# Order of work on VectorE and two value stages in a fused sorting attention and branch mixture, one core

## The chip, the core and the metric

One core of a Trainium2 chip runs the whole kernel. TensorE multiplies matrices into PSUM, VectorE (DVE), ScalarE (ACT) and GpSimd (POOL) do the elementwise work, and SyncE (SP) and GpSimd issue most DMAs. The metric is the device time of one execution in microseconds (us), as the median of several runs.

## The reference

Two parts follow each other. The first is an attention in which blocks of keys and values are first mixed by a matrix that five rounds of row and column normalization make from `sort_net`; the second is a mixture of four two-layer branches over the attention's output.

```python
P = sort_net                                     # 4 batches, 8 heads, 8 x 8
for _ in range(5):
    P = exp(P - max(P)); P = P / rowsum(P); P = P / colsum(P)
k_sorted = einsum('bhij,bhjcd->bhicd', P, k_blocks)
v_sorted = einsum('bhij,bhjcd->bhicd', P, v_blocks)
scores = q_blocks @ k_sorted_blocks.T / sqrt(64) # within each block of 96 tokens
attn = softmax(scores)
x = (attn @ v_sorted_blocks)                     # to (3072 tokens, 512)

p = domain_probs / domain_probs.sum(-1)          # 3072 x 4
out = 0
for e in range(4):
    h = maximum(x @ w1[e], 0)                    # 512 -> 1024
    out += p[:, e:e+1] * (h @ w2[e])             # 1024 -> 512
```

The inputs are q, k, v of shape 4 x 8 x 768 x 64 in fp32; the output is 3072 x 512 in fp32.

## The kernel before, in words

Matmuls run in fp16 and accumulate in fp32. Tokens are handled in twelve chunks of 256: three chunks (`c`) for each of the four batches (`b`). The second layer of a chunk, and for the last chunks the first layer too, is written as seven block products in place of eight (a Strassen-like scheme): sums and differences of blocks are made first (`h_sums`, numbers 1 to 4, on VectorE), the products accumulate in PSUM banks `bankA`, `bankB`, `bankC`, `bankQ`, and VectorE and ScalarE combine them.

The order of all instructions is written out by hand: each engine works through its own instructions in program order, and so does each engine that issues DMAs. The attention of the later batches is cut into stages that are called between pieces of the mixture. The table `PLANS[b]` says after which piece: an entry `(c, n, stage, batch, pair)` runs the stage in chunk `c` at slot `n`. Slots 0 to 5 of chunk (0, 2) follow the six groups of its first layer, slots 6 to 12 the products of its second layer. The stages are:

- `st_v(b, pr)` mixes the values of two heads on TensorE (line 361), ScalarE copies them (L367), and at every second pair six DMAs from SP write them to the tile `vs` (L375), from which `st_a` reads.
- `st_k` mixes keys (L395; ScalarE copies, L404, to `kT`); `st_q` transposes queries by a DMA from SP into `q_ring` (L383); `st_s` makes the scores (L414) and their exponential on ScalarE (L421).
- `st_a` multiplies by the values (L449), and VectorE normalizes (L430, L431). `st_x` transposes the result by a DMA from SP into `xT` (L465), a quarter of `xT` for each pair; the first layer of the next batch reads `xT`.
- `st_n`, `st_lk` and `st_lv` load queries, keys and values by GpSimd.
- `load_p` loads the weights of a chunk, `pb` (L213, SP).

A first layer of a chunk (`chunk_first`) is a row of groups of 16 matmuls (L780), each emptied by VectorE (L786). The attention's tiles in PSUM come from a pool of two buffers, which take turns.

Chunks 0 to 4 are made by `chunk`; the last seven by `last_first` and `last_second`, which use the seven products in the first layer too: the chunk G0 = 5 alone (`lead`), then three pairs. In `last_first` the seven products of a part use the PSUM tiles X, Z (two of each in turn) and Q. `p1` copies Z into X on ScalarE (L1124); `p2` adds a second product into Z, which `finish` empties on VectorE (L1110); `p6`, `p7` and `p4` go on adding into X, with ScalarE copies between (L1131, L1139), and X's last product (`p4`, `a22` by `t4`, the fourth) is emptied by `finish` too. Each turn of the loop makes the first products of part `e` (`now`) and the last ones of part `e - 1` (`prev`).

Of the kernel before, what the change touches and what calls it, by code (L numbers as in the profile page):

```python
# [12 lines left out]
ALU = mybir.AluOpType  # L13
# [4 lines left out]
def kernel(  # L18
# [18 lines left out]
    E = moe_w1.shape[0]  # L37
# [571 lines left out]
    def st_bk(b, qd):  # L609
# [10 lines left out]
            (1, 8, st_s, 1, 1), (1, 8, st_x, 1, 0), (1, 9, st_k, 1, 2), (1, 9, st_q, 1, 3), (1, 9, st_lv, 2, 1),  # L620
            (1, 11, st_a, 1, 1), (1, 12, st_lk, 2, 0),
            (2, 0, st_s, 1, 2), (2, 0, st_x, 1, 1), (2, 0, st_n, 2, 0), (2, 0, st_n, 2, 1), (2, 1, st_k, 1, 3),
            (2, 1, st_n, 2, 2), (2, 1, st_n, 2, 3), (2, 2, st_lk, 2, 1), (2, 3, st_a, 1, 2),
            (2, 4, st_x, 1, 2), (2, 4, st_q, 2, 0), (2, 5, st_s, 1, 3),
            (2, 5, st_q, 2, 1), (2, 6, st_a, 1, 3), (2, 7, st_v, 2, 0), (2, 8, st_x, 1, 3), (2, 8, st_v, 2, 1),
            (2, 9, st_k, 2, 0), (2, 9, st_lv, 3, 0), (2, 9, st_n, 3, 0), (2, 11, st_s, 2, 0), (2, 12, st_q, 2, 2),
        ],
        1: [
# [115 lines left out]
    def h_sums(e, which, own=False, hb=None):  # L744
        h = Hb[:, homes.get(e, e)] if hb is None else hb(e)
        blk = lambda kh, tok: h[:, ds(kh * KH, KH), ds(tok * P, P)]
        sm = [Sb[:, n, e].rearrange("p (f x) -> p f x", f=KH) for n in range(4)]
        tt = nc.vector.tensor_tensor
        if which == 1:
            tt(sm[0], blk(0, 1), blk(1, 1), ALU.add)  # L750
        elif which == 2:
            tt(sm[1], sm[0], blk(0, 0), ALU.subtract)
        elif which == 3:
            tt(blk(0, 1) if own else sm[2], blk(0, 0), blk(0, 1), ALU.subtract)
        else:
            tt(blk(1, 0) if own else sm[3], blk(1, 0), sm[1], ALU.subtract)

    def times(ps, lhs, rhs, es, first=True, done=True, between=None, at=None):

        for e in es:  # L760
            if e == at:
                between()
            for f in range(KH):
                nc.tensor.matmul(  # L764
                    ps, lhs(e, f), Ts[e][rhs][:, f, :],
                    start=(first and e == es[0] and f == 0), stop=(done and e == es[-1] and f == KH - 1),
                    skip_group_check=True,
                )
# [28 lines left out]
    def chunk(b, c, slot, done=()):  # L797

        es = list(range(E)) if b else list(range(1, E))
# [9 lines left out]
        sm = lambda n: (lambda e, f: Sb[:, n, e, ds(f * P, P)])  # L809
# [15 lines left out]
        p1, p5, u2, u3 = [moe.tile([P, DH], F32, name=f"{n}_{b}_{c}", tag=n, bufs=1) for n in ("p1", "p5", "u2", "u3")]  # L825
# [40 lines left out]
        if c:  # L866
            both = ob.rearrange("p (h d) -> p h d", h=2)
            times(bankA, blk(0, 0), "b11", es)
            slot()
            times(bankB, blk(1, 0), "b21", es)  # L870
            slot()
            tt(oa1, bankA, oa1, ALU.add)
            tt(oa1, bankB, oa1, ALU.add)
            h_sums(E - 1, 2)
            times(bankC, blk(1, 1), "n4", es[:1], True, False)
            times(bankQ, sm(0), "t1", es)
            tt(ob2, bankQ, ob2, ALU.add)
            slot()
            for e in es:
                h_sums(e, 3)  # L880
            for e in es:
                h_sums(e, 4)
            times(bankA, sm(1), "t2", es, False)
            tt(oa2, bankA, oa2, ALU.add)
            slot()
            next(sums0)
            times(bankC, blk(1, 1), "n4", es[1:], False)
            tt(ob1, bankC, ob1, ALU.add)
            slot()
            times(bankA, sm(2), "t3", es, False)  # L890
            tt(both, bankA.rearrange("p (o d) -> p o d", o=1).broadcast_to([P, 2, DH]), both, ALU.add)
            slot()
            store(1, ob)
            next(sums0)
            times(bankQ, sm(3), "b22", es, False)
            tt(oa2, bankQ, oa2, ALU.add)
            slot()
            store(0, oa)
            return
# [180 lines left out]
    def seven(g, n):  # L1080

        lead = g == G0
        if lead:
            e, f0, cols = n, 0, P
            pb = pbs[divmod(g, R // 2)]
            home = lambda i, j: Hb[:, e, ds(i * KH, KH), ds(j * P, P)]
            weight = lambda j: pb[:, ds(e, 1), ds(j * P, P)]
            n -= 1
            Q = last["Q"][(0, 0, 1, 3)[e]][:]
        else:  # L1090
            e, f0, cols = n // 2, n % 2 * 2, 2 * P
            home = lambda i, j: (last["H"][e] if j else Hb[:, e])[:, ds(i * KH + f0, 2), :]
            weight = lambda j: pbs[g](j, e)
            Q = last["Q"][n % 4][:]
        m = 512 // cols
        a, t = As[e], Bs[g]
        X, Z = [last[nm][n % len(last[nm])][:] for nm in ("X", "Z")]
        u2, u3, t22, t12 = [last[nm][n % len(last[nm])] for nm in ("u2", "u3", "t22", "t12")]
        tt = nc.vector.tensor_tensor

        def product(dst, lhs, rhs, first=False):
            for f in range(m):
                for k in range(2):
                    nc.tensor.matmul(  # L1104
                        dst[:, ds(f * cols, cols)], a[lhs][:, k, ds((f0 + f) * P, P)], t[rhs][:, k, :],
                        start=(first and f == 0 and k == 0), stop=(f == m - 1 and k == 1), skip_group_check=True,
                    )

        def finish(i, j, src):
            nc.vector.scalar_tensor_tensor(  # L1110
                out=home(i, j), in0=src.rearrange("p (f x) -> p f x", f=m), scalar=0.0,
                op0=ALU.max, in1=weight(j).broadcast_to([P, m, cols]), op1=ALU.mult,
            )

        def finish2(i, j, src):
            nc.scalar.activation(src, src, AF.Relu, bias=0.0, scale=1.0)  # L1116
            nc.gpsimd.tensor_tensor(  # L1117
                home(i, j), src.rearrange("p (f x) -> p f x", f=m),
                weight(j).broadcast_to([P, m, cols]), ALU.mult,
            )  # L1120

        def p1():
            product(Z, "a11", "b11", True)
            nc.scalar.copy(X, Z)  # L1124

        def p5():
            product(Q, "s1", "t1", True)

        def p6():
            product(X, "n2", "n2")  # L1130
            nc.scalar.copy(u2, X)  # L1131

        def p2():
            product(Z, "a12", "b21")
            finish(0, 0, Z)

        def p7():
            product(X, "s3", "t3")
            nc.scalar.copy(u3, X)  # L1139
            tt(t22, Q, u3, ALU.add)  # L1140

        def p4():
            product(X, "a22", "t4")
            finish(1, 0, X)

        def p3():
            product(Q, "s4", "b22")
            tt(t12, Q, u2, ALU.add)  # L1148

        return {  # L1150
            1: p1, 2: p2, 3: p3, 4: p4, 5: p5, 6: p6, 7: p7,
            22: lambda: finish2(1, 1, t22), 12: lambda: finish2(0, 1, t12),
        }

# [5 lines left out]
    def last_first(g, slot=None):  # L1160
        b, c = divmod(g, R // 2)
        lead = int(g == G0)
        if lead:
            chunk_first(b, c, [0], 0, slot)
            last_banks(0)
            last_tmp(g)
            prs = {1: seven(g, 1)}
            prs[1][1]()
            prs[1][5]()
            seven(g, 2)[5]()  # L1170
            prs[1][6]()
            prs[1][2]()
            input_sums(0, 0, True)
            input_sums(0, 1, True)
            last_banks(1)
        else:
            last["e0"][2]()
            prs = {0: last["e0"]}
        N7 = E if lead else 2 * E
        for e in range(1 + lead, N7):  # L1180
            prs[e] = seven(g, e)
        for e in range(1 + lead, N7):
            now, prev = prs[e], prs[e - 1]
            now[1]()
            prev[7]()
            if e > 1 + lead:
                prs[e - 2][12]()
            if not lead or e > 2:
                now[5]()
            now[2]()  # L1190
            now[6]()
            prev[22]()
            prev[4]()
            prev[3]()
        now[7]()
        prev[12]()
        return now

    def last_second(g, now=None, upper=False):

        b, c = divmod(g, R // 2)
        final = g == GN - 1
# [19 lines left out]
        def sums(e, which, own=False):  # L1222
            h_sums(e, which, own, hb)
# [24 lines left out]
            sums(e, 2)  # L1248
        product(bankC, blk(1, 1), "n4")
        nc.scalar.copy(ob1, bankC)  # L1250
        for e in range(E):
            sums(e, 4, True)
        if lead:
            for e in range(E):
# [8 lines left out]
        if not lead:  # L1263
            for e in range(E):
                sums(e, 3, True)
        early = 1 if final else 2
        for bank, part, _ in ends:
            product(bank[:, part], blk(1, 0), "b22", False, range(early), part=part)
        if closing and not final:
# [201 lines left out]
```

The softmax here doesn't subtract the row's maximum and nothing guards it: scores larger than these inputs give would overflow.

## Time and profile before

| what | us |
|---|---|
| median of 4 runs | 363.82 |
| lowest and highest run | 363.19 and 365.08 |
| the profiled execution | 364.28 |
| its span from first to last instruction | 362.5 |
| TensorE busy | 353.0 |
| VectorE busy | 272.0 |
| ScalarE busy | 172.6 |
| GpSimd busy | 133.6 |

Times in the trace count from the span's start. The granted TensorE clock was 1.000. In a list of waits, a line tells which engine and line waited for what: the sum, the number of times and the longest. In a timeline, a row has its start, its length, the engine, the line, the operation, the tiles (output, then inputs), and in brackets the idle time before it with what ended it. `SPq` marks the issue of a DMA, not its transfer; the time from issue to landing stands in the view of a tile. Where matmuls of one group are merged in a row, `x16` is their number. On the page, chunk (0, 2) runs from about 93.7 to 117.6, the first layer of batch 1's first chunk begins at 117.59, and the loop of the three pairs runs from about 209 to 234, 258 to 284 and 308 to 333.

### The profile page before, as it was taken

To read this page: it belongs to the slowest core of one execution; us is meant where nothing else is said; L and a number is where in the kernel's file an instruction comes from. 1 tells how busy PE (TensorE), PEld (TensorE's weight loads), DVE (VectorE), ACT (ScalarE), POOL (GpSimd) and SP (SyncE) were. 2 spreads that over 40 slices of the span, in tenths; PEclk is the share of its full clock that TensorE was granted. 3 is DMA by queue.
4 is the path that set the end of the run, shared out by engine and by line. 5 is a ranking of instruction groups with operands and counts; after the bars stand their busy time and mean duration, and the time that the engine had idled before them with its cause. 6 is when DMAs were issued, how large, how long until landed. Compare 5 with 4: busy or idle time off the path is not lost.

```text
span 362.5 us, 9496 instructions
## 1 busy us (share of the span) xinstructions
PE 353.0 (97%) x3949; PEld 305.7 (84%) x3949; DVE 272.0 (75%) x549; ACT 172.6 (48%) x306; POOL 133.6 (37%) x148
## 2 busy tenths in 40 slices
PE   8799999999999899999999999999999999999995
PEld 8685857888888788888889888888888888888895
DVE  5653897779798677868878977895587876677962
ACT  2664430452325255367937258830388611688210
POOL 8882010466112330000635318840068800288300
PEclk9999999999999999999999999999999999999999
DMA  8999999999998999935994310005200014100011
GB/s 115 203 207 229 214 209 198 203 182 201 217 124 144 186 128 162 174 75 74 172 205 72 109 68 0 2 2 127 95 13 2 3 56 120 61 0 2 2 72 46
DMA packets 72007, 40.52 MB, mean 112 GB/s; under 512 B 40598, under 2 KB 66716, under 8 KB 71964
## 3 DMA queue, kind: packets, MB, share of 16 engines
q0 software_dynamic: 36560, 19.93, 40.7%
q1 hardware_dynamic: 35260, 19.92, 27.4%
q8 instruction: 31, 0.51, 0.6%
q14 instruction: 12, 0.10, 0.1%
q10 hardware_dynamic: 144, 0.07, 0.1%
HBM read 42.13 MB, written 6.34 MB: 134 GB/s over the span
## 4 chain that ended last, share of the span: by engine, by line
PE 87%; DVE 5%; DMA 4%; ACT 1%; issue 1%; POOL 1%; ACTq 0%; DVEq 0%
PE ps_h L780 17%; PE ps_Q L1217 17%; PE ps_p L764 10%; PE ps_X L1104 10%; PE ps_Z L1104 7%; PE ps_Q L1104 7%; PE ps_Z L1217 6%; DMA w<-in_moe_w_dram 4%; PE ps_o L704 3%; PE ps_p L815 3%; PE ps_h L669 1%; PE ps_s L414 1%; PE ps_a L449 1%; PE ps_v L361 1%; PE ps_k L395 1%
## 5 line engine op out<-in xcount | busy, mean ns | idle before, releaser
L780 PE MATMUL ps_h<-xT,w 128*128 128x256 f16 x576 | 67.7, 273 | 0.0
L780 PEld LDWEIGHTS <-w 128*128 128x128 f16 x576 | 55.2, 98 | 7.3
L786 DVE SCALAR_TENSOR_TENSOR Hb<-ps_h,pb 128x1024 f16<-128x1024 f32 x34 | 41.5, 1224 | 17.3 <-PE ps_h L780 17.1
L1104 PEld LDWEIGHTS <-w 128*128 128x128 f16 x480 | 43.5, 98 | 6.4 <-issue 0.3
L1117 POOL TENSOR_TENSOR arena<-tmp,pb 128x512 f16<-128x512 f32 x12 | 15.3, 1274 | 65.8 <-PE ps_Z L1104 49.9
L1217 PEld LDWEIGHTS <-Hb 128*128 128x128 f16 x320 | 31.2, 98 | 3.5
L1116 ACT ACTIVATE tmp<-tmp 128x512 f32<-128x512 f32 x46 | 29.3, 637 | 3.2 <-DVE tmp L1148 2.6
L1217 PEld LDWEIGHTS <-Sb 128*128 128x128 f16 x304 | 28.2, 98 | 3.0
L1104 PEld LDWEIGHTS <-arena 128*128 128x128 f16 x312 | 27.7, 98 | 2.9
L421 ACT ACTIVATE ET<-ps_s 96x768 f16<-96x768 f32 x24 | 18.1, 802 | 25.4 <-PE ps_s L414 25.1
L404 ACT CAST kT<-ps_k 64x384 f16<-64x384 f32 x48 | 22.7, 473 | 14.1 <-PE ps_k L395 13.1
L121 POOL DMA_DIRECT2D arena<-in_q_dram x24 | 19.9, 843 | 18.0 <-DMA q_ring<-arena 17.2
L1104 PE MATMUL ps_X<-ET,arena 128*128 128x256 f16 x168 | 25.2, 272 | 0.0
L1124 ACT COPY ps_X<-ps_Z 128x512 f32<-128x512 f32 x27 | 15.4, 570 | 19.8 <-PE ps_Z L1104 15.6
L764 PEld LDWEIGHTS <-Hb 128*128 128x128 f16 x232 | 21.9, 98 | 3.0
L1217 PE MATMUL ps_Q<-w,Hb 128*128 128x256 f16 x192 | 24.4, 273 | 0.0
L1104 PE MATMUL ps_Z<-xT,w 128*128 128x256 f16 (+1 forms) x176 | 22.5, 257 | 0.2 <-ACT ps_X L1124 0.2
L1140 DVE TENSOR_TENSOR tmp<-ps_Q,tmp 128x512 f32<-128x512 f32 x20 | 13.8, 691 | 11.3 <-ACT tmp L1139 7.6
L1110 DVE SCALAR_TENSOR_TENSOR Hb<-ps_X,pb 128x512 f16<-128x512 f32 x27 | 18.4, 681 | 1.5 <-PE ps_X L1104 1.5
L1131 ACT COPY tmp<-ps_X 128x512 f32<-128x512 f32 x26 | 15.2, 586 | 9.0 <-PE ps_X L1104 8.7
L750 DVE TENSOR_TENSOR Sb<-Hb 128x512 f16<-128x512 f16 x33 | 19.5, 609 | 0.0
L1110 DVE SCALAR_TENSOR_TENSOR Hb<-ps_Z,pb 128x512 f16<-128x512 f32 x27 | 18.4, 682 | 1.3 <-PE ps_Z L1104 1.3
(261 smaller groups left out, 744.0 us busy)
## 6 DMA issues: line engine op xcount, KB each, us to landing
w<-in_moe_w_dram POOLq DMA_DIRECT2D x7, 1024.0 KB, 27.5
pb<-p_dram SPq DMA_DIRECT2D x9, 512.0 KB, 6.5
arena<-in_k_dram POOLq DMA_DIRECT2D x8, 384.0 KB, 9.1
arena<-in_v_dram POOLq DMA_DIRECT2D x8, 384.0 KB, 7.4
vs<-arena SPq DMA_DIRECT2D x36, 66.0 KB, 5.3
arena<-in_q_dram POOLq DMA_DIRECT2D x24, 96.0 KB, 8.2
out_dram<-ob SPq DMA_DIRECT2D x9, 256.0 KB, 2.1
out_dram<-oa SPq DMA_DIRECT2D x8, 256.0 KB, 2.3
```

Of the source, the lines that this page charges most:

```text
L121: nc.gpsimd.dma_start(t[:, h // 2, :, h % 2, :], q[b, h].rearrange("(t p) d -> p t d", p=P))
L404: nc.scalar.copy(kT[ds(D * hh, D), r], pk[ds(D * r, D), hh].rearrange("p a (i c) -> p a i c", c=CP),)
L421: nc.scalar.activation(ETs[2 * (pr % 2) + hh][:, 0:S].rearrange("c (a x) -> c a x", a=2), pss[hh][0:BLK, :, 0:HS], AF.Exp, bias=0.0, scale ...
L750: tt(sm[0], blk(0, 1), blk(1, 1), ALU.add)
L764: nc.tensor.matmul(ps, lhs(e, f), Ts[e][rhs][:, f, :], start=(first and e == es[0] and f == 0), stop=(done and e == es[-1] and f == KH - 1 ...
L780: nc.tensor.matmul(ps[:, f, :], w1sb[e][:, kc, ds((4 * g + f) * P, P)], xT[:, kc, ds(2 * c * P, 2 * P)], start=(kc == 0), stop=(kc == NKC ...
L786: nc.vector.scalar_tensor_tensor(out=Hb[:, homes.get(e, e), ds(4 * g, 4), :], in0=ps[:], scalar=0.0, op0=ALU.max, in1=weights(e).broadcast ...
L1104: nc.tensor.matmul(dst[:, ds(f * cols, cols)], a[lhs][:, k, ds((f0 + f) * P, P)], t[rhs][:, k, :], start=(first and f == 0 and k == 0), st ...
L1110: nc.vector.scalar_tensor_tensor(out=home(i, j), in0=src.rearrange("p (f x) -> p f x", f=m), scalar=0.0, op0=ALU.max, in1=weight(j).broadc ...
L1116: nc.scalar.activation(src, src, AF.Relu, bias=0.0, scale=1.0)
L1124: nc.scalar.copy(X, Z)
L1217: nc.tensor.matmul(ps, lhs(e, f), Ts[e][rhs][:, f, part], start=(first and e == 0 and f == 0), stop=(e == E - 1 and f == KH - 1), skip_gro ...
```

## The change

It has four parts. In `PLANS[0]` the stages `st_v(2, 0)` and `st_v(2, 1)` are called in chunk (0, 2) at slots 2 and 4, in its first layer, in place of slots 7 and 8, in its second; at slot 4 `st_v(2, 1)` stands between `st_x(1, 2)` and `st_q(2, 0)`. In `chunk`, for the chunks (0, 1) and (0, 2), the product with `t2` and VectorE's addition from its bank come ahead of the fourth sums. In `last_first`, for the three pairs, VectorE empties X of the part before ahead of Z of the present part; the product into Z stays at its place. In `last_second`, outside the lead chunk, the fourth sums are made at the old place only for the branches that are used early (two, or one in the final chunk), and for the others after the third sums.

```diff
@@ PLANS[0]
-            (2, 1, st_n, 2, 2), (2, 1, st_n, 2, 3), (2, 2, st_lk, 2, 1), (2, 3, st_a, 1, 2),
-            (2, 4, st_x, 1, 2), (2, 4, st_q, 2, 0), (2, 5, st_s, 1, 3),
-            (2, 5, st_q, 2, 1), (2, 6, st_a, 1, 3), (2, 7, st_v, 2, 0), (2, 8, st_x, 1, 3), (2, 8, st_v, 2, 1),
+            (2, 1, st_n, 2, 2), (2, 1, st_n, 2, 3), (2, 2, st_lk, 2, 1), (2, 2, st_v, 2, 0), (2, 3, st_a, 1, 2),
+            (2, 4, st_x, 1, 2), (2, 4, st_v, 2, 1), (2, 4, st_q, 2, 0), (2, 5, st_s, 1, 3),
+            (2, 5, st_q, 2, 1), (2, 6, st_a, 1, 3), (2, 8, st_x, 1, 3),
@@ chunk, chunks (0, 1) and (0, 2)
             for e in es:
                 h_sums(e, 3)
+            times(bankA, sm(1), "t2", es, False)
+            tt(oa2, bankA, oa2, ALU.add)
             for e in es:
                 h_sums(e, 4)
-            times(bankA, sm(1), "t2", es, False)
-            tt(oa2, bankA, oa2, ALU.add)
             slot()
@@ seven
+        def p2_first():
+            product(Z, "a12", "b21")
+
+        def p2_last():
+            finish(0, 0, Z)
...
-            1: p1, 2: p2, 3: p3, 4: p4, 5: p5, 6: p6, 7: p7,
+            1: p1, 2: p2, 3: p3, 20: p2_first, 21: p2_last, 4: p4, 5: p5, 6: p6, 7: p7,
@@ last_first
-            now[2]()
+            now[2 if lead else 20]()
             now[6]()
             prev[22]()
             prev[4]()
+            if not lead:
+                now[21]()
             prev[3]()
@@ last_second
-        for e in range(E):
+        early = 1 if final else 2
+        for e in range(E if lead else early):
             sums(e, 4, True)
...
         if not lead:
             for e in range(E):
                 sums(e, 3, True)
-        early = 1 if final else 2
+            for e in range(early, E):
+                sums(e, 4, True)
```

## The prediction

> **What bounds the kernel now.** The page comes first: TensorE is busy for 97% of the span, and its row of slices shows nines nearly everywhere after the first twentieth. Time can only come from short holes in TensorE's stream, so the next view is who TensorE waited for.
>
> ```profile
> span 362.5 us, 9496 instructions
> PE 353.0 (97%) x3949; PEld 305.7 (84%) x3949; DVE 272.0 (75%) x549; ACT 172.6 (48%) x306; POOL 133.6 (37%) x148
> ```
>
> ```profile
> PE ps_a L449 <- issue: 1.4, 1, 1.4
> ...
> PE ps_p L764 <- DVE room L884: 0.3, 1, 0.3
> ```
>
> "Issue" means that the profile names no releaser. The timeline gives the place: 124.77, the first `st_a` of batch 2. It needs `vs`, which the SP queue fills with six DMAs; the last, issued at 116.79, took 7.9 us to land: 124.7. That is the releaser. The timeline of TensorE, and the view of the tile `vs` for the last two DMAs:
>
> ```profile
> 121.75 1.58 PE L780 MATMUL ps_h<-xT,w 128*128 128x256 f16 x13
> 124.77 0.64 PE L449 MATMUL ps_a<-vs,ET 96*128 96x65 f16 x16 [1.43 <-issue]
> ```
>
> ```profile
> L375 SPq DMA_DIRECT2D vs<-arena x2: 624/626/627, 116.1 to 116.8; - x2
> ...
> DMA to landing us min/median/max: 6.7/7.3/7.9
> ```
>
> A matmul is written as 0.27 us but the next one starts 0.11 later, so a hole costs its idle time plus 0.16: 1.60 here, 0.48 at L884.
>
> The SP queue before that hole, in order: a transpose of `xT`, two of `q_ring`, the weights `pb` of the next chunk, the last transpose of `xT` of batch 1 (`st_x(1, 3)`), then `vs`.
>
> ```profile
> 104.98 1.21 SPq L465 DMA_TRANSPOSE xT<-xsl  x1
> 106.36 3.31 SPq L383 DMA_TRANSPOSE q_ring<-arena  x2
> 109.77 0.54 SPq L213 DMA_DIRECT2D pb<-p_dram  x1
> 110.41 1.22 SPq L465 DMA_TRANSPOSE xT<-xsl  x1
> 112.76 4.66 SPq L375 DMA_DIRECT2D vs<-arena  x6
> ...
> 117.59 1.91 PE L780 MATMUL ps_h<-xT,w 128*128 128x256 f16 x16
> ```
>
> The last row is the first matmul of batch 1: its fourth (117.92) reads what `st_x(1, 3)` wrote, and it did not wait.
>
> In the seven-product part the chain shows a small regular loss: the second product into Z takes 0.55 instead of 0.44.
>
> ```profile
> 225.20 0.44 PE ps_Q L1104 x4
> 225.64 0.55 PE ps_Z L1104 x4
> ```
>
> The timeline of the other engines tells why:
>
> ```profile
> 226.76 0.68 DVE L1110 SCALAR_TENSOR_TENSOR Hb<-ps_Z,pb 128x512 f16<-128x512 f32 x1
> 227.35 0.68 DVE L1110 SCALAR_TENSOR_TENSOR Hb<-ps_X,pb 128x512 f16<-128x512 f32 x1
> 228.14 0.57 ACT L1124 COPY ps_X<-ps_Z 128x512 f32<-128x512 f32 x1 [0.29 <-DVE Hb L1110]
> ```
>
> ScalarE's copy into X waits until VectorE has emptied X, which stands behind the emptying of Z; TensorE then waits for the copy (228.14 + 0.57 = 228.71, Z at 228.76). (By the timeline the Z products start at 225.59 and 228.76.) The loop ACT L1124, ACT L1139, DVE L1140, DVE Z, DVE X, ACT L1124 takes 3.17 us (224.97 to 228.14), while 28 matmuls at 0.109 take 3.06.
>
> **The change part by part.**
>
> (1) Order of the two evacuations. X's product starts at 226.46, lasts 0.60, and VectorE can take it at about 227.16 (ScalarE starts 0.1 after a product ends). VectorE would be done at 227.84; the copy's other input, Z, is ready at 227.34 + 0.60 + 0.1 = 228.04. So the copy starts 0.1 earlier, the Z product finds it done (228.61 against 228.65 in an unbroken stream), and the loop is broken. Behind the X evacuation now come Z (to 228.45) and L1148 (to 229.1); L1140 of the next step is wanted at 229.2, so VectorE still fits, with 0.1 us to spare. Z's result goes to `Hb`, read only in the second layer; at the pair's end it is wanted at 235.9 and ready by 234.5. Loss per pair from the timeline's Z starts: 0.04, 0.05, 0.12, 0.12, 0.12 = 0.45; three pairs 1.35. Some hundredths will stay: −1.3, with ends −1.4 and, if VectorE's small margin fails, 0.
>
> (2) `tt(oa2, …)` ahead of the fourth sums in chunk (0, 1). TensorE's next accumulation into the same bank waits for L884, which stands behind three L756 (1.09 us). Moved up, it ends at 89.5, before TensorE arrives at 90.07. The fourth sums end at 90.5 and are read from 91.9: hidden, 1.4 us to spare. −0.48. In chunk (0, 2) the same hole is 0.17, but the next `st_s` needs ScalarE's `kT`, done at 115.60, and TensorE arrived at 115.73: only −0.06 is real.
>
> (3) Order of sums in `last_second`. No hole there belongs to VectorE. The one wait, 0.2 at 355.45 for the third sums' product, ends with ScalarE's copy L1262 (355.03 + 0.37). The delayed fourth sums now end where the third ended (244.94, 255.78 and 354.5) and are wanted at 246.38, 259.48 and 357.19: hidden with over 1.4 us. 0. Were that cover gone, the four or so of 0.33 us each would show.
>
> (4) The two `st_v`. Two matmuls each (0.33 us), one ScalarE copy (0.80) and, after the second, six DMAs are moved, none is added. TensorE's sum is unchanged. ScalarE is idle at both new places (its `kT` copies end at 100.26). The first needs `PIv`, built at 79.67, and a load issued at 77.91, which lands 7.4 us later by the median: both there. The second `st_v` comes one group after `st_a(1, 2)` and takes the PSUM buffer that VectorE frees at 104.12 + 0.33, while TensorE gets there at 103.93 + 0.33: a new hole of about 0.28 (ends 0 and 0.4), with the chunk's last first-layer group behind it. GpSimd's load of V for batch 3, held until 112.19 by the second `st_v`, can start about 7 us earlier; the query loads behind it wait for `q_ring` and move to about 115.5; their users come over 10 us later. 0.
>
> The gain: the last `vs` DMA is issued at about 109.5 and lands between 114 and 117 (4.3 to 7.5 us in the other two rounds that the trace shows), wanted at 123: the hole of 1.60 is gone.
>
> The price is on the SP queue. The six `vs` DMAs wait for ScalarE's copy, done at about 105.9 when SP arrives at 106.2, so that is no new wait, but they now stand ahead of two `q_ring` transposes, `pb` and `st_x(1, 3)`. With part 2's 0.48, the first `xT` transpose is issued at 104.98 + 0.33 − 0.48 = 104.83; `vs` from 106.2 to 110.1 (3.9 as at 134.8; the two issue starts of the last pair lie 0.63 apart); the two transposes to 112.8 at 1.21 each with gaps; `pb` to 113.4; `st_x(1, 3)` at 113.5, 3.1 us later than now. TensorE wants it at 117.92 + 0.28 − 0.48 − 0.06 = 117.66. Does it land in 4.2 us?
>
> The rows for this transpose:
>
> ```profile
> DMA to landing us min/median/max: 2.8/6.1/9.6
> ```
>
> 2.8 was one with an empty queue before it. Here ten DMAs stand close before it, with `pb` directly ahead, which took 6.5 in this place, 8 elsewhere. I take 6.8: landing at 120.3, a hole of 2.6 at the first group of batch 1. The Trainium skill, "DMA: Bandwidth & Descriptors", section "Latency and other measured facts", would say otherwise: first byte at 0.6 us and 261 GB/s for a DMA transpose, so 1.4 us for these 192 KB, landing near 115 and no hole. Three rows contradict that price; the same page's "Queues, rings and completion order" has each DMA engine consume descriptors in ring order, so a transfer pays for those ahead. By the first rule the sum is −3.2, by the rows −0.6. I take the rows; ends of the hole 0 and 5.3. `pb` lands about 0.7 earlier and its reader waits behind the delayed group: nothing more. The first `q_ring` transpose, issued at 110.2, lands at 115 to 116.5 (4.7 in its old place), wanted by `st_s(2, 0)` at 115.6: a hole there of up to 1 us would come out of the 2.6, since `st_x(1, 3)` lands when it lands.
>
> **The sum.** −1.3 − 0.48 − 0.06 + 0.28 − 1.60 + 2.6 = −0.56. The profiled execution took 364.28 (span 362.5) and would take 363.7; it lies 0.46 above the median of the four runs, 363.82, so the median goes to 363.3.
>
> **The rivals.**
>
> The queue catches up. `st_x(1, 3)` lands within 4.2 us, no new hole: −3.2, 360.6. For it: the 2.8 row, and the V load no longer competes at 116. Against: `pb` directly ahead. It counts as over 0.5% faster once the hole is below 1.3 us.
>
> The queue chokes: slower. In the like sequence of batch 1 (`vs`, `pb`, then a `q_ring` transpose at 139.4) the issue took 2.9 us and the landing 10.1. If `st_x(1, 3)` takes that, it lands at 123.6, a hole of 5.9, sum +2.7, 366.5. It decides from a landing at 122.7. For it: issues back up when the queue is full (1.93 and 3.1 us for one transpose). Against: the place now measured took 4.7 for transposes.
>
> The evacuation order does nothing: Z's evacuation or L1148 becomes the late one and the period stays 3.17. Then part 1 gives 0 and the sum is +0.7, 364.5. VectorE's sum of 2.6 in a period of 3.06 speaks against it.
>
> **How the numbers follow.** A measurement of this kernel can tell about 0.5%, 1.8 us. Forecast (hole 1.3 to 5 us, with or without part 1): 0.57. Catches up: 0.26, faster. Chokes: 0.17, slower. The range takes the hole from 0.3 to 5.3 with 0.5 for the scatter of runs: 360.9 to 366.0; the likeliest case alone (hole 1.5 to 4.1) 362.2 to 364.8.
>
> **What would show it.** Right: no hole at the first `st_a` of batch 2; a new one of some us within the first four matmuls of batch 1, with the releaser a DMA of `xT`; no L884 wait near 90; Z starts 3.06 apart in the pairs; the `vs` row on SP ahead of the `q_ring` row. Wrong: `xT` landing before 117.7, Z starts still 3.17 apart, or a new wait of TensorE in `last_second`.

## The result and the profile after

| | median us | runs | range |
|---|---|---|---|
| before | 364.01 | 56 | 362.56 to 372.01 |
| after | 365.83 | 35 | 363.24 to 368.47 |

The ratio after to before is 1.0056, 95% interval 1.0044 to 1.0069. The prediction was 363.3, 0.5 below before; it is 1.8 above. Here and below, medians are over all executions of a kernel, while ratios leave out the few that took over 1.5% more than the fastest of the same kernel.

The profiled execution of after took 363.24 (span 361.5). That is the fastest of all its executions, so its trace shows the steps but not the typical time. Two lines of its page, TensorE's busy time and its costliest group, whose last columns are the idle time before it and the releaser:

```profile
span 361.5 us, 9496 instructions
...
PE 352.2 (97%) x3949; PEld 306.2 (85%) x3949; DVE 274.4 (76%) x549; ACT 172.9 (48%) x306; POOL 133.4 (37%) x148
...
L780 PE MATMUL ps_h<-xT,w 128*128 128x256 f16 x576 | 68.2, 273 | 2.7 <-DMA xT<-xsl 2.7
```

Its list of waits of TensorE. The entries for L449 and L884, which stood here before, are gone; two others have come, and nothing of `last_second` is among them:

```profile
PE ps_h L780 <- DMA xT<-xsl: 2.7, 1, 2.7
...
PE ps_v L361 <- DVE xsl L431: 0.3, 1, 0.3
```

Their places, in the timeline of TensorE in after:

```profile
103.62 0.50 PE L361 MATMUL ps_v<-arena 128*128 128x384 f16 x2 [0.26 <-DVE xsl L431]
...
120.14 1.58 PE L780 MATMUL ps_h<-xT,w 128*128 128x256 f16 x13 [2.68 <-DMA xT<-xsl]
```

The second is the hole that the prediction named: three matmuls of batch 1's first group, then the wait for `st_x(1, 3)`, 13 matmuls after it. With the 0.16 that a written hole lacks it is 2.85. SP's issues ahead of it:

```profile
104.43 1.22 SPq L465 DMA_TRANSPOSE xT<-xsl  x1
105.74 3.78 SPq L375 DMA_DIRECT2D vs<-arena  x6
109.63 3.08 SPq L383 DMA_TRANSPOSE q_ring<-arena  x2
112.80 0.54 SPq L213 DMA_DIRECT2D pb<-p_dram  x1
113.43 1.23 SPq L465 DMA_TRANSPOSE xT<-xsl  x1
```

The last issue was predicted for 113.5 with a landing at 120.3; it came at 113.43 and landed at 120.10. The close match of the issue is luck in part: the first transpose went out 0.4 earlier than predicted (104.43 in place of 104.83), and the two transposes of queries took 0.5 longer (3.08 in place of 2.6). In the pairs VectorE takes X ahead of Z, and ScalarE's copy waits for the product into Z alone:

```profile
227.62 0.69 DVE L1110 SCALAR_TENSOR_TENSOR Hb<-ps_X,pb 128x512 f16<-128x512 f32 x1 [0.27 <-PE ps_X L1104]
...
228.23 0.68 DVE L1110 SCALAR_TENSOR_TENSOR Hb<-ps_Z,pb 128x512 f16<-128x512 f32 x1
228.54 0.57 ACT L1124 COPY ps_X<-ps_Z 128x512 f32<-128x512 f32 x1 [0.16 <-PE ps_Z L1104]
```

The Z products start 3.06 apart (221.74, 224.80, 227.85, 230.91). So every step shows where it was predicted, and this execution is 1.04 below the profiled one of before. What is missing is in the other executions. For each of them the mean granted clock is on record. Of 36 executions of after, 7 have 0.997 or more, called full clock below (median 364.29), 24 about 0.995 (366.02), 5 have 0.992 or less (367.51). Of 59 of before, taken beside the first experiments, 54 have 0.997 or more. The trace above, at 0.999, is one of the seven.

### The profile page after: what moved, and what is told of

Read it like the earlier page. It is cut to its first block, busy times and chain, and to the rows that moved or that the text cites. A ratio compares the mean times of both kernels' runs of the same rounds, so it can differ in the third digit from the quotient of the medians.

```text
span 361.5 us, 9496 instructions
## 1 busy us (share of the span) xinstructions
PE 352.2 (97%) x3949; PEld 306.2 (85%) x3949; DVE 274.4 (76%) x549; ACT 172.9 (48%) x306; POOL 133.4 (37%) x148
## 4 chain that ended last, share of the span: by engine, by line
PE 90%; DVE 4%; DMA 2%; ACT 2%; issue 1%; ACTq 0%; DVEq 0%
PE ps_Q L1225 17%; PE ps_h L780 17%; PE ps_p L764 10%; PE ps_X L1104 10%; PE ps_Z L1104 7%; PE ps_Q L1104 7%; PE ps_Z L1225 6%; PE ps_h L669 3%; PE ps_o L704 3%; PE ps_p L815 3%; DMA xT<-xsl 2%; PE ps_s L414 1%; PE ps_a L449 1%; PE ps_v L361 1%; PE ps_k L395 1%
## 5 line engine op out<-in xcount | busy, mean ns | idle before, releaser
L750 DVE TENSOR_TENSOR Sb<-Hb 128x512 f16<-128x512 f16 x33 | 20.5, 639 | 0.0
L1154 DVE TENSOR_TENSOR tmp<-ps_Q,tmp 128x512 f32<-128x512 f32 x26 | 17.7, 681 | 0.8 <-PE ps_Q L1104 0.8
```

## The experiments

All ratios are to the kernel before, with 95% intervals.

**Parts apart.** e1 is after with the two `st_v` back at their old slots (parts 1 to 3); e2 is before with `st_v` moved (part 4 alone); e9 is before with the order of evacuation alone (part 1).

```diff
 e1, against after
-(2, 2, st_v, 2, 0), (2, 4, st_v, 2, 1)
+(2, 7, st_v, 2, 0), (2, 8, st_v, 2, 1)
 e2, against before: the same the other way round
 e9, against before: only the edits in seven and last_first
```

> The changed kernel with the two value stages back at slots 7 and 8: parts 1 to 3 alone. Three theories of why the changed kernel is 0.56% slower though its profiled execution is 1.0 us faster. GATE: the new 2.8 us hole of TensorE at the first group of batch 1 lets the granted clock drop in most executions (mean 0.995 or 0.991 instead of 0.999) and that costs about another 2 us. QUEUE: in most executions xT lands later than in the profiled one, so the hole itself is 4 to 6 us. ORDER: VectorE's new order costs something in the pairs that the one profile hides. GATE and QUEUE: 1.8 us below before (1.3 in the pairs, 0.48 at chunk (0, 1)), ratio 0.995, mean clock as before, and the 1.60 us hole at the first st_a of batch 2 is there. ORDER: at or above before, ratio 1.000 to 1.003.

> The kernel before with nothing but the two value stages moved to slots 2 and 4. GATE: hole of about 2.6 us in place of the 1.60, plus 0.3 at the second value stage, makes 1.3 us, and the clock drops in most executions for about 2 us more: 3.3 to 4 us above before, ratio 1.009 to 1.011, mean clock 0.995. QUEUE: the same time, with a hole of 4 to 6 us and a mean clock at 0.999. ORDER: only 1 to 1.5 us above before, ratio 1.003 to 1.004.

> The kernel before with VectorE's order of the two evacuations alone (part 1). By the prediction's step: Z starts 3.06 us apart instead of 3.17, 1.3 us below before, ratio 0.9964. If VectorE's small margin made the other evacuation the late one: ratio 1.000 and Z starts still 3.17 apart.

| | median us | ratio | executions at full clock |
|---|---|---|---|
| e1 | 362.46 | 0.9946 (0.9928 to 0.9963) | 17 of 22 |
| e2 | 367.49 | 1.0086 (1.0057 to 1.0115) | 2 of 6 |
| e9 | 362.74 | 0.9957 (0.9943 to 0.9972) | 22 of 22 |

Parts 1 to 3 are worth 1.88 (364.34, before's median beside e1, to 362.46), part 1 alone 1.47. Part 4 makes the loss, alone too. The trace of e1 has no hole at the first `st_a` of batch 2, though SP's order there is that of before: the hole of 1.60 is not in every execution.

The trace of e2 has the hole, and what comes after it. TensorE in e2, then two windows of its trace. In these the columns are the window, its length, the busy time of TensorE, of its weight loads, VectorE, ScalarE and GpSimd (with counts), then the granted clock, DMA share and GB/s:

```profile
121.25 2.54 PE L780 MATMUL ps_h<-xT,w 128*128 128x256 f16 x13 [2.38 <-DMA xT<-xsl]
```

```profile
118.27:121.69 3.42, 1.04 (x11) 0.79 (x9) 0.42 (x1) 0.46 (x1) 0.00 (x0) 1.00 1.50 127
121.69:125.10 3.41, 3.41 (x22) 2.61 (x20) 1.27 (x2) 0.56 (x2) 0.36 (x1) 0.50 0.94 267
```

TensorE stood for 2.54 until 121.25; from 121.69 to 125.10, 3.41 us, the clock is at one half, and some 22 matmuls run where 31 would, 0.109 apart. The wait that took the place of the old one has a second price.

**Once more.** Further profiled executions, one of before and two of after.

> The kernel before once more, for one further trace. The two kernels whose SP order is that of before (parts 1 to 3 alone, and the evacuation order alone) showed no hole at the first st_a of batch 2. If the 1.60 us hole of the profiled execution is the exception and not the rule: a hole of 0 to 0.5 us here, and a span about 1 us below 362.5. If it is the rule: 1.6 us again.

> The changed kernel once more, for a further trace; 29 of its 36 executions had a mean clock of 0.995 or less. GATE: a hole of 2.5 to 3.5 us at the first group of batch 1, and if the mean clock is 0.995 a stretch of some 3.4 us at half clock begins within 3 us of the hole's end and costs 1.4 to 1.7 us against the first trace of this kernel. QUEUE: a hole of 4 us or more and a full clock.

> The changed kernel a third time, with the same expectations: GATE a hole of 2.5 to 3.5 us, followed or not by a stretch at half clock; QUEUE a hole of 4 us or more.

e6 (363.63) has a hole of 0.79 at the first `st_a` of batch 2, where before's own trace has 1.60. e7 (366.98) and e7b (366.30) have holes of 3.41 and 3.86 at the first group of batch 1, half clock for 3.41 us in both. TensorE in e7b:

```profile
121.83 2.93 PE L780 MATMUL ps_h<-xT,w 128*128 128x256 f16 x13 [3.69 <-DMA xT<-xsl]
```

e7 also waits earlier, for queries. TensorE in e7:

```profile
116.71 0.52 PE L414 MATMUL ps_s<-q_ring,kT 64*128 64x96 f16 x16 [1.12 <-DMA q_ring<-arena]
...
122.22 2.84 PE L780 MATMUL ps_h<-xT,w 128*128 128x256 f16 x13 [3.24 <-DMA xT<-xsl]
```

The 13 matmuls took 1.58 in after's trace and take 2.84 here. SP in e7:

```profile
106.06 4.18 SPq L375 DMA_DIRECT2D vs<-arena  x6
110.35 4.88 SPq L383 DMA_TRANSPOSE q_ring<-arena  x2
115.32 0.53 SPq L213 DMA_DIRECT2D pb<-p_dram  x1
115.95 1.24 SPq L465 DMA_TRANSPOSE xT<-xsl  x1
```

Behind the `vs` DMAs the two transposes of queries took 4.88 to issue, in place of 3.08, so `st_x(1, 3)` came 2.5 later than in after's trace.

**Another place for the six DMAs.** e4 leaves the matmuls and copies of `st_v` at slots 2 and 4, but issues the `vs` DMAs behind `st_x(1, 3)`; e5 issues them from ScalarE; e8 leaves them and puts `pb` behind `st_x(1, 3)`; e10 is e4 with the second `st_v` at slot 7, where its PSUM buffer is free.

```diff
 e4, against after (st_vd: the six DMAs of st_v(2, 1))
-(2, 8, st_x, 1, 3),
+(2, 8, st_x, 1, 3), (2, 8, st_vd, 2, 0),
 e5, against after, with st_vd on ScalarE's queue
-(2, 6, st_a, 1, 3),
+(2, 6, st_vd, 2, 0), (2, 6, st_a, 1, 3),
 e8, against after (st_p: load_p of the next chunk)
-(2, 8, st_x, 1, 3),
+(2, 8, st_x, 1, 3), (2, 8, st_p, 1, 0),
 e10, against e4
-(2, 4, st_v, 2, 1),
+(2, 7, st_v, 2, 1),
```

> The changed kernel with the six vs DMAs issued only behind st_x(1, 3) at slot 8; the matmuls and the copy of the two value stages stay at slots 2 and 4. SP's order is then that of before. xT lands at about 116.6, no hole at the first group of batch 1. The vs DMAs can start at once behind st_x (about 111.2 instead of 112.8 in the kernel before), so the last lands some 1.1 us earlier and the hole at the first st_a of batch 2 is 0.5 to 1.0 us instead of 1.60. GATE and QUEUE: parts 1 to 3 (-1.8), the new 0.4 at the second value stage, -0.8 at st_a: 2.2 us below before, ratio 0.994, clock 0.999 to 1.000. ORDER: above 0.998.

> The changed kernel with the six vs DMAs issued by ScalarE at slot 6 (it sits idle from about 107.9 to 113.2) in place of SP at slot 4. SP's order is that of before, nothing stands newly ahead of st_x(1, 3). GATE and QUEUE: xT lands before 117.7, no hole at the first group of batch 1 and none at the first st_a of batch 2; six issues of 0.6 us on ScalarE end at about 111.7, so its kT copies are not late. Parts 1 to 3 minus the 0.4 at the second value stage: at least 1.5 us below before, as the kernel with the vs DMAs behind st_x (ratio 0.994), full clock in 9 of 10 executions. If the DMA engines rather than SP's order are what delays xT, the vs packets still compete with it and some of the hole stays: ratio 0.998 or more.

> The changed kernel with the weights pb of the next chunk loaded behind st_x(1, 3) in place of ahead of it; the vs DMAs stay ahead of both. If pb directly ahead is what makes st_x(1, 3) take 6.7 us: it lands some 3 to 4 us earlier, at 116 to 117, the hole at the first group falls from 2.8 to under 0.5 us; pb, issued 1.3 us later, lands near 120.5, VectorE's first evacuation waits for it and TensorE gets a hole of about 1 us at the third group, too short for the clock to drop. Time 1.5 to 3.5 us below the changed kernel, ratio to before 0.996 to 1.001, full clock in most executions. If the whole queue is the cause and not its order: xT lands as late as in the changed kernel, ratio 1.0056, and the clock drops in 8 of 10 executions.

> The changed kernel with the first value stage at slot 2, the second back at slot 7, and the vs DMAs behind st_x(1, 3) at slot 8: a version meant to beat both. The 0.42 us hole of the second value stage at slot 4 goes, since VectorE has freed its PSUM buffer at slot 7, and the vs DMAs still start when SP has issued st_x(1, 3). All theories: 0.4 us below the kernel with both at slots 2 and 4 and the vs DMAs behind, near 360.9, ratio 0.993. If the copy on ScalarE comes later than SP, the vs DMAs start later and the hole at st_a comes back in part: ratio 0.994 to 0.996.

| | median us | ratio | executions at full clock |
|---|---|---|---|
| e4 | 361.34 | 0.9941 (0.9919 to 0.9962) | 19 of 22 |
| e5 | 365.38 | 1.0016 (0.9993 to 1.0039) | 7 of 22 |
| e8 | 364.48 | 1.0009 (0.9990 to 1.0028) | 12 of 22 |
| e10 | 364.72 | 1.0009 (0.9986 to 1.0031) | 13 of 22 |

e4 is the fastest of all. SP there:

```profile
106.29 2.73 SPq L388 DMA_TRANSPOSE q_ring<-arena  x2
109.13 0.52 SPq L213 DMA_DIRECT2D pb<-p_dram  x1
110.44 1.75 SPq L470 DMA_TRANSPOSE xT<-xsl  x1
112.28 3.85 SPq L380 DMA_DIRECT2D vs<-arena  x6
```

and TensorE, without a wait at either place, the first group of batch 1 and the first `st_a` of batch 2:

```profile
117.45 1.91 PE L785 MATMUL ps_h<-xT,w 128*128 128x256 f16 x16
...
123.03 0.65 PE L454 MATMUL ps_a<-vs,ET 96*128 96x65 f16 x16
```

The last `vs` DMA is issued at 115.49 and lands at 122.36, just ahead of its reader. So the loss goes when the six DMAs stand behind `st_x(1, 3)`; the earlier compute alone is harmless, but for the 0.42 at the PSUM buffer, which stays.

e5 was expected to be as fast as e4 and is not. The DMAs hold ScalarE, where copies of keys stand behind them. ScalarE, then TensorE, in e5:

```profile
108.88 8.59 ACTq L380 DMA_DIRECT2D vs<-arena  x5
117.50 1.96 ACT L409 CAST kT<-ps_k 64x384 f16<-64x384 f32 x4 [8.01 <-DMA vs<-arena]
```

```profile
118.53 0.21 PE L419 MATMUL ps_s<-q_ring,kT 64*128 64x96 f16 x1 [1.68 <-ACT kT L409]
119.52 0.51 PE L419 MATMUL ps_s<-q_ring,kT 64*128 64x96 f16 x15 [0.78 <-ACT kT L409]
```

And `st_x(1, 3)` is late here too, though SP has none of the six DMAs. In e5 it was issued at 111.59 and landed 9.2 later, at 120.76, past the 117.9 at which TensorE reads it in before:

```profile
L470 SPq DMA_TRANSPOSE xT<-xsl x1: 2039/2039/2039, 111.6 to 111.6; - x1
...
DMA to landing us min/median/max: 9.2/9.2/9.2
```

So it is not SP's order alone: with the six transfers sent from another queue, three ahead of it and three behind, it is late as well.

In e8 `st_x(1, 3)`, without `pb` ahead of it, landed in 2.9 us (114.08 to 116.95), and the first group didn't wait; but `pb` landed at 123.09, and TensorE waited at the third group for VectorE, which reads it:

```profile
124.47 3.02 PE L783 MATMUL ps_h<-xT,w 128*128 128x256 f16 x16 [2.62 <-DVE Hb L789]
```

In e10 SP issues `st_x(1, 3)` at 110.23, as early as in before, and still TensorE waits for it:

```profile
120.66 2.93 PE L785 MATMUL ps_h<-xT,w 128*128 128x256 f16 x13 [3.12 <-DMA xT<-xsl]
```

GpSimd had issued three loads in the same time, in e10:

```profile
110.08 0.74 POOL L110 DMA_DIRECT2D arena<-in_v_dram  x1 [8.65 <-PE ps_v L361]
111.39 1.73 POOL L121 DMA_DIRECT2D arena<-in_q_dram  x2 [0.56 <-DMA q_ring<-arena]
```

**GpSimd's load of V.** This suggested a theory: the second `st_v` holds that load, it starts 7 us earlier in after (104.42), and the prediction had put that at nothing. e11 is after with the load moved into the next chunk; e14 is e10 and e15 is e1 with the same.

```diff
-(2, 9, st_lv, 3, 0)          # chunk (0, 2)
+(0, 1, st_lv, 3, 0)          # chunk (1, 0)
```

> The kernel after, with one stage moved: GpSimd's load of V for batch 3 (st_lv(3, 0)) goes from chunk (0, 2), where the earlier second st_v lets it start at about 104.5 us, to the next chunk, behind the key differences st_n(3, 0). SP's order stays that of after, with the vs DMAs ahead of the last xT transpose. If the V load is what makes the queue late: the first xT transpose lands in 3 to 4.5 us, st_x(1, 3) at 117.5 to 119, the hole at the first group of batch 1 is under 1 us, half clock becomes rare, 361.5 to 363, ratio 0.993 to 0.998. If SP's order alone makes it: hole still 2.5 us or more, clock reduced in most executions, 365.5 to 366.5, ratio 1.004 to 1.006.

> A candidate for the best plan: parts 1 to 3; the two st_v at slots 2 and 7 (no PSUM buffer hole at slot 4), the vs DMAs behind st_x(1, 3) as before the change, GpSimd's V load for batch 3 later as in e11. If the V load is what broke the same plan in e10 (hole 3.28 at the first group): no hole there and none at the first st_a of batch 2, 360.5 to 361.5, ratio 0.991 to 0.994. If the queries that move up with it compete as well: a hole of 1 us or more and 362 to 365.

> Parts 1 to 3 with the two st_v in their old places (e1) and GpSimd's V load later. The old vs DMAs land late in some executions only, and the V load of GpSimd was issued beside them. If it is what makes them late: about 361.5 to 362, ratio 0.992 to 0.994, a little below e1, with full clock in nearly all executions. If not: as e1, 0.9946.

| | median us | ratio | executions at full clock |
|---|---|---|---|
| e11 | 368.40 | 1.0107 (1.0072 to 1.0143) | 0 of 6 |
| e14 | 362.80 | 0.9964 (0.9949 to 0.9980) | 21 of 22 |
| e15 | 362.23 | 0.9940 (0.9917 to 0.9963) | 12 of 12 |

For after the theory fell: with the load out of the way of the first transpose it is no faster, by these six executions slower still. SP in e11 (half clock from 16.9 to 23.8 has put this trace some 3.7 later; why it came there was not found):

```profile
108.14 1.22 SPq L465 DMA_TRANSPOSE xT<-xsl  x1
109.45 4.85 SPq L375 DMA_DIRECT2D vs<-arena  x6
114.41 2.62 SPq L383 DMA_TRANSPOSE q_ring<-arena  x2
117.12 0.54 SPq L213 DMA_DIRECT2D pb<-p_dram  x1
117.76 1.23 SPq L465 DMA_TRANSPOSE xT<-xsl  x1
```

The first transpose now lands in 2.8 us, where it took 6.2 in after. But SP issues `st_x(1, 3)` 9.62 after it, no sooner than in after (9.00), and now V (119.30), behind the queries (117.68, 118.49), goes out beside it: it lands 8.0 later, and TensorE in e11 shows

```profile
125.82 2.65 PE L780 MATMUL ps_h<-xT,w 128*128 128x256 f16 x13 [4.65 <-DMA xT<-xsl]
```

For e10's plan the load does matter: with V issued at 112.97, behind the queries, in place of 110.08 ahead of them, the hole at the first group is gone in e14's trace, and the time falls from 364.72 to 362.80. It stays above e4 because the other hole, which was expected to be gone too, is back. TensorE in e14, whose last `vs` DMA landed at 124.32:

```profile
124.41 0.64 PE L454 MATMUL ps_a<-vs,ET 96*128 96x65 f16 x16 [1.58 <-issue]
```

In e15 nothing is gained over e1. What rides beside a transfer decides when it lands; when `st_x(1, 3)` is issued is decided by SP's order.

**The price of half clock.** e3 is after with 22 needless matmuls in the hole; e3b is the same kernel once more.

```diff
 e3, in the first group of chunk (1, 0)
+for _ in range(22):
+    nc.tensor.matmul(ps[:, 0, :], w1sb[0][:, 0, 0:P], w1sb[0][:, 1, 0:2 * P], start=True, stop=True)
```

> The changed kernel with 22 needless matmuls of 256 columns (2.4 us at 0.109 each) put ahead of the first group of batch 1, into the same PSUM bank, whose contents the group then overwrites: they lie in the hole and wait for nothing new. xT lands when it did, so the hole of 2.8 us is cut to some 0.45 us but the group starts at the same time. GATE: the clock stays at 0.999 to 1.000 in all executions, and the kernel is about 2 us faster than the changed one, near 363.3 or slightly below before (ratio to before 0.997 to 1.000). QUEUE: the same time as the changed kernel, ratio to before 1.0056, a hole of 2 to 3 us beside the dummies in slow executions. ORDER: 1.0056.

> The kernel with 22 needless matmuls in the hole once more: it kept the full clock in 21 of 22 executions and yet was only 0.15% faster than the changed kernel, where GATE wanted 0.5%. If xT lands later there than in the first trace of the changed kernel (QUEUE in part): first group resumes more than 5.4 us after the first st_s(2, 0), against 4.94 in that trace. If the needless matmuls cost time elsewhere: it resumes after 4.9 to 5.1 us and the loss lies behind it.

e3 took 365.59, ratio 1.0041 (1.0024 to 1.0057). The clock was full in 21 of 22 executions, and from the end of the hole to the first matmul of `st_s(2, 1)` TensorE needs 9.74, as in the trace of after, against 11.39 in e7 and e2 and 11.10 in e7b; and yet the time hardly fell. The hole had stayed, in e3:

```profile
117.33 2.56 PE L780 MATMUL ps_h<-w 128*128 128x256 f16 x22
119.73 0.49 PE L785 MATMUL ps_h<-xT,w 128*128 128x256 f16 x3
121.15 1.58 PE L785 MATMUL ps_h<-xT,w 128*128 128x256 f16 x13 [0.93 <-DMA xT<-xsl]
```

22 matmuls (2.4) and 1.10 of idle time make 3.5. e3b (368.57) had 3.3 there and 2.17 at `st_s(2, 0)`.

So a pause was made by hand in the plan of e4, which has no late transfer: e17 idle, by eight ScalarE copies in the group's PSUM tile that the first matmul waits for; e19 by 32 matmuls. e18 was to be the twin of e17 with the copies and matmuls side by side.

```diff
 e17, in the first group of chunk (1, 0), against e4
+nc.tensor.matmul(ps[:, 0, :], w1sb[0][:, 0, 0:P], w1sb[0][:, 1, 0:2 * P], start=True, stop=True)
+for _ in range(8):
+    nc.scalar.copy(ps[:, 3, :], ps[:, 0, :])
 e18: the same with the copies from ps[:, 2, :], and 30 more such matmuls behind them
 e19: 32 such matmuls, no copies
```

> The plan of e4 (no hole at the first group of batch 1), with a hole made by hand there: one needless matmul into the group's PSUM buffer and eight needless ScalarE copies inside it, which the group's first matmul has to wait for. 8 copies at 0.372 us (256 columns, by the profile) and the hand-over make about 3.2 us in which TensorE is idle, with nothing late in the queues. If a hole costs half clock on top of itself: e4's 361.3 + 3.3 + most of 1.5 = 365.5 to 366.2, mean clock about 0.995 in most executions, ratio 1.004 to 1.006. If a hole costs itself alone: 364.6, ratio 1.001, clock full.

> The twin of e17: the same eight copies on ScalarE, but TensorE doesn't wait for them; it runs 31 needless matmuls in the same place, 31 x 0.109 = 3.4 us. The clock stays full: e4's 361.3 + 3.4 = 364.7, ratio 1.001 to 1.002. If half clock after a hole is worth 1.5 us in most executions, e17 is 1 to 1.5 us above this; if the clock is worth nothing to the time, both are equal.

> The twin that e18 was meant to be, without copies on ScalarE: the plan of e4 with 32 needless matmuls ahead of the first group of batch 1, 32 x 0.109 = 3.5 us, where e17 has a hole of 3.33 + 0.1 us. If the time of e17 is the hole and half clock: e4's 361.3 + 3.5 = 364.8, the same as e17's executions at full clock (364.9) and 1.1 below its others (366.0), clock full in nearly all executions. If filling the hole doesn't help, 366.0.

| | median us | ratio | at full clock | at about 0.995 |
|---|---|---|---|---|
| e17 | 365.94 | 1.0040 (1.0024 to 1.0056) | 6 executions, 364.88 | 15 executions, 366.03 |
| e19 | 365.06 | 1.0034 (1.0015 to 1.0052) | 20 executions, 365.00 | 2 executions |

TensorE in e17, and its clock, with the window columns as above:

```profile
117.38 0.27 PE L784 MATMUL ps_h<-w 128*128 128x256 f16 x1
...
120.81 2.73 PE L791 MATMUL ps_h<-xT,w 128*128 128x256 f16 x16 [3.16 <-ACT ps_h L788]
```

```profile
118.31:121.72 3.41, 0.91 (x9) 0.81 (x9) 0.00 (x0) 2.26 (x7) 0.00 (x0) 1.00 1.21 247
121.72:125.14 3.42, 3.42 (x22) 2.62 (x20) 1.56 (x2) 0.89 (x2) 0.65 (x1) 0.50 0.30 71
```

A pause of 3.33 with nothing late in a queue lowers the clock in 16 of 22 executions, and those at 0.995 take 1.15 more than those at full clock. With only six of the latter the size is rough; resampling the executions gives 0.3 to 2.0. Filled with matmuls the pause costs little more than its own length (3.7 over e4 in the medians, 4.1 each against its own before, for 32 matmuls of 0.109, 3.5 in all) and no clock. The medians of e17 and e19 differ by 0.9; each against its own before, by 0.5, which is not clear of noise. So that half clock costs time is shown within e17, and its size is about one microsecond.

e18 (370.49, ratio 1.0162, 1.0137 to 1.0188) was no twin: its matmuls write the tile that the copies read and waited for them too, so it had the pause and the matmuls one after the other. It tells nothing on the clock's price.

**When half clock comes.** The traces also show what decides it. Each holds records of the granted clock, with the time at which each begins; the first lies between 4.06 and 6.89 us after the span's start. Counted from there, half clock at the first groups of batch 1 began 34 times 3.413 us later in e2, e7, e7b, e10, e17 and e18 and 35 times in e8 and e11, to a hundredth of that unit (e2: 5.63 and 121.69; e17: 5.67 and 121.72). The time from the hole's end to it was anything between −0.6 us (e7b) and 1.0 (e18). So the clock is set anew for each of a row of windows of 3.413 us, and these don't start with the hole. What counts is the idle time within one window. In e2 and e17 above, the window ahead of half clock has 2.4 and 2.5 us of it. After's hole, longer than that of e2, lay across two windows, 1.09 in one and 1.60 in the other:

```profile
115.13:118.55 3.42, 2.33 (x33) 1.85 (x32) 1.76 (x4) 1.52 (x3) 0.70 (x1) 1.00 0.84 127
118.55:121.96 3.41, 1.81 (x20) 1.66 (x20) 0.20 (x1) 0.00 (x0) 0.00 (x0) 1.00 1.56 232
121.96:125.37 3.41, 3.41 (x34) 3.06 (x32) 2.85 (x3) 1.90 (x4) 3.00 (x4) 1.00 0.86 165
```

From 30 to 340 us it holds for all twenty traces: eight windows had 2.4 us or more of idle time, and each was followed by one window at half clock; no other had more than 1.7, and none of those was. An estimate from these bounds: a pause of 3.33 that falls anywhere in the windows puts 2.4 us into one of them in 6 cases of 10, and 1.7 in nearly all; 16 of 22 lies between. The half clock near 17 us in e11 does not fit (the window before it has 1.3 of idle time); there the matmuls are small ones.

## Why the prediction was wrong

| term | predicted | measured |
|---|---|---|
| part 1 | −1.3 | −1.47 (e9) |
| parts 1 to 3 | −1.84 | −1.88 (e1) |
| PSUM buffer at slot 4 | +0.28 | +0.42 (trace of after) |
| hole at the first `st_a` of batch 2, gone | −1.60 | 1.60, 0.79, 0, 0, 1.32 in five traces with SP's old order (before, e6, e1, e9, e15) |
| new hole at the first group of batch 1 | +2.6 | 2.85, 3.41 (and 1.28 ahead), 3.86, 2.54 in four traces with the new order: 3.5 |
| half clock after it | not in the sum | 1.15 in 29 of 36 executions: 0.9 |

The forecast's mechanism was right and is shown: six DMAs ahead of `st_x(1, 3)` on SP make it late (e2 against before, e4 against after), and in the profiled execution the hole came to within 0.25 of the forecast. Parts 1 and 2 came out as worked out; the stretch in chunk (0, 1) that holds the L884 wait is 0.48 shorter. Part 3 has no run of its own; it brought no new wait. Of the rivals, the order of evacuation is out by e9. The queue that catches up is out: of the four traces with the new order none has the transpose there in time. The queue that chokes is what e7 begins to show, at 4.7 us of holes; it was priced at 5.9.

The sum has its terms right in kind and one missing. With the measured mean hole of 3.5 in place of 2.6 it would still have said +0.34, too little to tell from nothing. The stated range, 360.9 to 366.0, is that of the hole alone; the 0.5 for the scatter of runs is not in it.

Three steps failed.

First, "a hole costs its idle time plus 0.16". The prediction asked what is late behind the hole and found nothing; it did not ask what the pause does to TensorE, and put that at nothing without a reason, though its range of holes went up to 5.3. e17 shows the price by itself, 1.15 for one window at half clock, and 29 of 36 executions of after have at least one: 0.9. A rule for it stands in the Trainium skill, "TensorE: Matmul & The Clock Gate", "Part 1: The HAM clock gate": the clock has two states, full and one half, and is set by a free-running window of 3413 ns. The traces agree: half clock for 3.41 us each time, on a grid of 3.413 that doesn't move with the hole. Its section "Why this matters for your kernels" wants pauses to stay under some 3 us. A 2.6 us hole would pass by that. Here 2.54 (e2) was followed by half clock and 2.85 (after) was not; by the windows above, what decides is whether 2.4 of it fall into one.

Second, the issue times on SP. The prediction gave the two transposes of queries 1.21 each with gaps, 2.6 in all, and so 8.67 from the issue of the first `xT` transpose to that of `st_x(1, 3)`. The four traces took 9.00, 8.97, 9.39 and 11.20, 9.64 in the mean; the two transposes alone took 3.0 to 4.9. (The row of before that the prediction shows has 3.31 for them.) The landing was priced right: 6.8 against 6.67, 6.89, 7.29 and 6.22. So the mean hole is 3.5, with e7's extra 1.28, and not 2.6. Why the issues vary is not shown. In the two traces where they took longest, e7 and e3b (11.69), GpSimd's load of keys had gone out 1.2 to 1.3 us ahead of the first transpose; in after, e2, e7b and e3 (9.39) it was 3.0 to 4.8 ahead. The prediction's zero for the earlier V load had no trace behind it, but that load is not what makes after slow: in e4 it goes out as early (104.90), and e4 is the fastest.

Third, the gain of 1.60 was the size of one execution. The five traces have 0.74 on average; e4's median is 1.12 below e1's in spite of its 0.42, which would make the old hole worth 1.5, but the two are not apart by their intervals. The runs leave it between 0.7 and 1.5.

The sum by the measured terms: −1.88 + 0.42 + 3.5 + 0.9 less 0.7 to 1.5 gives +1.4 to +2.2; measured +1.82. By the difference of e4 and after, 4.5 in the medians and 4.2 by the ratios, the new hole and its half clock come out the same: 3.5 + 0.9 is 4.4.

What stays open: e3, at full clock, should by this lie 3.5 above e4 and lies 4.25. Its two traces (e3 and e3b) have further holes of 0.4 to 1.0 between 165 and 188, before which the profile names copies of ScalarE, and which those of after don't have; why was not found. Also open is whether the price is nearer the 1.15 of e17's executions or the 1.65 that its trace loses between the hole and `st_s(2, 1)`, as e7 and e2 do.

The version that beats both kernels is e4, 0.9941; e1 and e15, and by their intervals e9 and e14, can't be told from it.

## What to carry to other kernels

A stage that is moved earlier takes its DMAs with it; e4 shows that compute and transfers can be moved apart, and that the transfers belong behind the one that is wanted first. Where TensorE is nearly always busy, price a new hole at its length, and from about 2.4 us on at the half clock that may follow as well, and weigh that against several small gains. A hole that waits for a DMA has one size in one profiled execution: take its size from several before counting on its going or coming.

## What was not expected of the hardware

A transfer's time depended on the other queues, whoever issued it: the first `xT` transpose, 192 KB, took 2.8 us in e11, 6.2 in after, where V was issued at the same moment, and 9.2 in e7, where V was too and queries and keys had gone out 2.9 and 1.3 us before. V is not all: in e15 it came 10 us later, with queries and keys 2.5 and 0.9 ahead, and the transpose took 7.6. The Trainium skill, "DMA: Bandwidth & Descriptors", "Issuing engines are not separate DMA queues", says as much: DMAs of all issuing engines run on the same 16 DMA engines. e5 adds that an engine that issues DMAs can lose more than the issue: ScalarE worked on nothing else for 8.0 us, until its last DMA was issued.

The two states of the clock sort the executions of one kernel into groups: 364.29, 366.02 and 367.51 in after. A profile of the fastest execution showed a kernel faster than before, while the median was slower. And the clock is decided by idle time within fixed windows of 3.413 us: a hole of 2.54 cost half clock and one of 2.85 did not.
